# A scan-and-mixer kernel: the sums of WQ's columns in two rounded products, ten preparatory products, the order made anew

## The chip, the cores and the metric

The kernel runs on one core of a Trainium2 chip. The core has five queues that matter here: TensorE (PE in the profile, with its weight loads as PEld), VectorE (DVE), ScalarE (ACT), GpSimd (POOL, which also issues the accumulating transfers) and SyncE (SP, which issues the other transfers). The metric is the device time of one execution in microseconds. Before the change it is 519.17 us, the median of 3 runs from 518.96 to 519.18.

## The reference

```python
x  = A_x                                # 1 x 2048 x 512, float32
xn = layernorm(x)                       # eps 1e-5
# A: linear attention, 32 heads of 16
q, k, v = heads(xn @ wqkv)
phi = lambda t: where(t > 0, t + 1, exp(t)) + 1e-6
pq, pk = phi(q), phi(k)
kv  = einsum("bhsd,bhse->bhde", pk, v);  z = einsum("bhsd->bhd", pk)
s   = (einsum(pq, kv) / (einsum(pq, z)[..., None] + 1e-6)) @ wo
# B: spatial-shift mixer, then an MLP 512 -> 1376 -> 512
h   = gelu(layernorm(xn) @ w1)
x1  = xn + shifted(h) @ w2              # four channel groups, shifted by +1, -1, +2, -2
m   = x1 + gelu(layernorm(x1) @ w3) @ w4
return x + s * silu(m)
```

All inputs and the output are float32. The products have to be more exact than one product of rounded operands gives.

## The kernel before, in words

Rows are tiled by 128, so there are 16 row tiles; four of them make a block, and there are four blocks. Columns and inner dimensions are cut into chunks of 128 (four for 512).

TensorE has two kinds of product. A native float32 product (`slow=True` in `mm`, line 141) runs in two passes. A rounded product takes operands of type float32r. To keep the precision, an operand is split into a rounded part `hi` and a rest `lo`: `rounded` (line 478) is one ACT copy into `hi` and one VectorE subtraction into `lo`. A product of two split operands is then three rounded products, hi with hi, hi with lo and lo with hi (`products`, line 470).

The layer norm ahead of wqkv isn't applied to the rows before the product. The raw rows, transposed on the host, are multiplied, and the mean is corrected afterwards: `sums` (line 680) adds the four chunks of a weight matrix with three VectorE additions into one tile t, multiplies a matrix of ones by t, which leaves the sums of all columns in every row of a PSUM bank, and an ACT copy negates them into `wneg` (for the keys) or `qneg` (for the queries). The first step after each product of rows and weights is then `t = wneg * mean + product` (`feature_k`, line 739, and `query`, line 765) on VectorE, and ACT scales by the inverse deviation. W1's columns are centered in a like way by `center` (line 561), whose sum is already taken in two rounded products.

The work runs in this order. Preparatory products (`warm`, line 1168) use TensorE until the first weights land. Then come the keys of block 0 (the first two tiles with a native product of the unrounded first chunk), the sums of WK's columns, the load and split of WQ, the sums of WQ's columns, and from there queries, keys, and `gram` (line 776), which accumulates the keys' features against the normalized rows in four PSUM banks. The halves of a key's features and of its normalized rows are k0h, k0l, x0h, x0l and so on. For the mixer, `mix1` multiplies shifted blocks by w1, `mix2` multiplies by w2 in the form of `seven` (line 783), which gets a 2x2 block product from seven products instead of eight, with VectorE additions between them. Behind row tile 15 the attention matrices are closed, and then the MLP runs block by block: `up_pair` in sevens, `down` into four accumulator banks (`acc`), the attention's products in sevens (`attend_pair`), and `gate` at the block's end. The rows of y, which feed `up_pair`, go through DRAM to be turned: `Turned.put` stores them, `Turned.take` fetches them in four transfers per half block (line 715).

None of this order is the order of execution. Each operation is entered in a plan with an estimated duration, and `emit` (line 267) writes out all five queues by simulating them: it takes the next operation by its due time (`deadlines`, `backward`), gives tiles their buffers, and assumes transfer times. What it writes is static; on the chip each queue runs in the order written and waits where an operand isn't there. The numbers that steer it are these: the allowance for a transfer in the due time (6.0 us plus 4 us per MB, line 265), `SAFE` (line 230), the margin that a reader gets behind the assumed landing of its transfer, `lead` and `reserve` (in the call of line 1409), how early a tile of a class may be taken and how many free ones lengthen that, and `SOONER` (line 1401), a table of pairs: operation number, and by how many quarters of a microsecond its due time is brought forward. Operation numbers count the operations in the order entered, so an operation that is added moves the numbers behind it.

There are four PSUM banks for products (`mm`) and four for accumulators (`acc`), and 90 buffers of class "p" in SBUF for most of the tiles.

Of the kernel before, what the change touches and what calls it, by code (L numbers as in the profile page):

```python
# [85 lines left out]
class Plan:  # L86
# [140 lines left out]
    GAP = .06  # L227
    PATIENCE = 2.5
    COLD, COLD_TILL = 1.84, 5.8
    SAFE = 2.0  # L230
    early = 0.0
    patience = 18.0

# [27 lines left out]
    def backward(self):  # L261
        for op in reversed(self.ops):
            if op.eng != "PE":
                for o in op.post:
                    op.due = min(op.due, o.due - self.GAP - (6.0 + op.mb * 4 if op.mb else op.lat))

    def emit(self, first, lead, reserve, window, ahead, table=()):
        self.deadlines(first)
# [19 lines left out]
        while left:  # L288
# [86 lines left out]
            for o in op.post:  # L375
# [7 lines left out]
                if op.mb:  # L383
                    r = max(r, min(r + self.SAFE, o.due + slip - o.lat - self.SAFE))
                o.ready = max(o.ready, r)
# [8 lines left out]
def linear_attn_gated_by_mixer(  # L394
# [24 lines left out]
    W = 4  # L419
    SHIFT = (-1, 1, -2, 2)  # L420
    ORDER = (0, 2, 1, 3)
    WARM = 8
    PIECE = BT + W
    EARLY = (), ()
    AHEAD = 30.0, 20.0, 10.0, 0.0, 0.0
# [12 lines left out]
    pl = Plan(nc, pools, counts, ("acc", "mm"))  # L438

    def piece(name, dt=F32):  # L440
        return pl.new("p", name, dt, PIECE)[:, :512]

    def rounds(name):

        return piece(name + "h", F32R), piece(name + "l", F32R)
# [4 lines left out]
    def bank(name):  # L450
        return pl.new("mm", name, F32, 512)[:, :]

    def fixed(name, n, dt=F32):

        t = pl.new("const", name, dt, n)
        t.ap = const.tile([P, n], dt, name=name)
        return t
# [9 lines left out]
    def split(out, full, hi):  # L467
        pl.tt(out, full, hi.f32, ALU.subtract)
# [9 lines left out]
    def rounded(hi, lo, full, src=None):  # L478

        pl.act(hi, src or full, AF.Copy)  # L480
        split(lo, full, hi)
# [9 lines left out]
    ident, ones, nhalf, zacc = fixed("ident", P), fixed("ones", P), fixed("nhalf", QT), fixed("zacc", 512)  # L491
    identr = fixed("identr", P, F32R)
    onesr, bmask, tiny, zmore = fixed("onesr", P, F32R), fixed("bmask", P), fixed("tiny", 1), fixed("zmore", 1)
# [186 lines left out]
    def sums(w, ps, out):  # L680

        t, r = piece(f"{w.name}t"), w.raw
        pl.tt(t, r[0], r[1], ALU.add)
        pl.tt(t, t, r[2], ALU.add)
        pl.tt(t, t, r[3], ALU.add)
        pl.mm(ps, ones.all, t, True, True, slow=True)
        pl.act(out, ps, AF.Copy, scale=-1.0)


# [478 lines left out]
    warm = bank("warm")  # L1168
    for n in range(WARM):
        pl.mm(warm.cols(n % NC * P, (n % NC + 1) * P), ones.all, ones.all, True, True, slow=True)  # L1170
# [18 lines left out]
    WK = Weights("wk", wqkv[1])  # L1189
# [17 lines left out]
    for i in range(2):  # L1207
        project(ks[i], i, WK, [3])
    sums(WK, ksum, wneg)
    for i in range(2):  # L1210
        feature_k(i, ks[i])
# [3 lines left out]
    WQ = Weights("wq", wqkv[0])  # L1215
    WQ.split()
    sums(WQ, bank("qsum"), qneg)
    query(0)
    gram(0)
# [77 lines left out]
    for base, s in ((0, 1), (DH - 1, -1)):  # L1297
        v = bmask.all.via(lambda ap: ap.rearrange("p (h d) -> p h d", d=DH))
# [16 lines left out]
    for gg in range(NC):  # L1315
        cs = gg * P, (gg + 1) * P
        ps = bank(f"kv{gg}").cols(0, P)
# [4 lines left out]
    for gg in range(NC):  # L1322
        ps = bank(f"m{gg}")
# [10 lines left out]
    for b in range(NQ):  # L1334
# [46 lines left out]
        else:  # L1381
# [3 lines left out]
            t = piece(f"xi{i}", F32R)  # L1385
# [13 lines left out]
                gate(b * QT + QT - 1, a, o, D // 2, late=True, by_dma=False, whole=o > 0)  # L1399

    SOONER = (
# [6 lines left out]
    )  # L1408
    pl.emit(first=6.0, lead={"p": 14.0, "w": 14.0, "ab": 10.0}, reserve={"p": 20, "w": 1, "ab": 0}, window=12.0,
            ahead=6.0, table=SOONER)  # L1410


# [35 lines left out]
```

## Time and profile before

| what | value |
|---|---|
| median of 3 runs | 519.17 us (518.96 to 519.18) |
| profiled execution | 519.35 us, of it 517.6 us span |
| mean granted TensorE clock | 0.998 |
| busy: TensorE / weight loads | 511.2 / 445.0 us |
| busy: VectorE / ACT / POOL | 394.0 / 324.8 / 102.8 us |
| DMA | 100.12 MB, mean 193 GB/s |

The span runs from the first to the last instruction; the rest of the profiled execution's time lies around it. A product on TensorE is shown with its whole passage through the array, so that successive products overlap in the profile: a busy TensorE doesn't tell that it runs at its peak, and a short gap doesn't show in the busy time. The distance from one start to the next does. The two passes of a native product are two instructions. In the rows of the timeline and of the chain the first number is the start in us, the second the duration; an arrow reads "out from in"; a bracket tells how long the engine was idle before and who ended that.

### The profile page before, as it was taken

How to read it: one execution, taken by the hardware profiler on the slowest of the kernel's cores; microseconds unless marked ns; L12 is line 12 of the kernel's file. 1: busy time of each engine (PE TensorE's matmuls, PEld its weight loads, DVE VectorE, ACT ScalarE, POOL GpSimd, SP SyncE). 2: the span in 40 equal slices, each digit the busy share in tenths (PEclk: the TensorE clock that was granted, in tenths of full speed). 3: DMA queues.
4: the chain of work that ended last, by engine and by line, in shares of the span. 5: the costliest groups of instructions: out<-in, count | busy, mean ns of one | idle time of the engine just before them, and what ended most of it. 6: DMA issues, size and time to landing. Idle time of an engine off the chain costs nothing.

```text
span 517.6 us, 8927 instructions
## 1 busy us (share of the span) xinstructions
PE 511.2 (99%) x3005; PEld 445.0 (86%) x3005; DVE 394.0 (76%) x788; ACT 324.8 (63%) x664; POOL 102.8 (20%) x195
## 2 busy tenths in 40 slices
PE   8999999999999999999999999999999999999996
PEld 6777888988888888898889989899898898999985
DVE  5884987569567838999999999655886657895635
ACT  5899784579558657787866755345453545535621
POOL 1378643431363022211100001000020000200000
PEclk9999999999999999999999999999999999999999
DMA  8759994375976389989767759648488376687604
GB/s 277 255 101 248 225 205 97 74 172 182 220 169 162 68 185 249 259 261 262 287 200 225 237 175 249 212 152 208 133 214 276 122 201 157 179 248 225 243 1 122
DMA packets 73281, 100.12 MB, mean 193 GB/s; under 512 B 7844, under 2 KB 30900, under 8 KB 73236
## 3 DMA queue, kind: packets, MB, share of 16 engines
q1 hardware_dynamic: 63876, 82.52, 50.6%
q0 software_dynamic: 9360, 17.04, 19.9%
q8 instruction: 23, 0.38, 0.3%
q14 instruction: 22, 0.18, 0.1%
HBM read 60.33 MB, written 30.81 MB: 176 GB/s over the span
## 4 chain that ended last, share of the span: by engine, by line
PE 91%; ACT 5%; DVE 2%; DMA 1%; issue 1%; SPq 0%; DVEq 0%
PE acc L146 22%; PE pb L146 10%; PE k L146 8%; PE h L146 8%; PE q L146 7%; PE g L146 7%; PE pe L146 5%; PE pbs L146 5%; PE pbm L146 4%; PE pa L146 3%; PE pes L146 2%; PE a L146 2%; PE pem L146 2%; PE pas L146 1%; ACT y L167 1%; PE pam L146 1%
## 5 line engine op out<-in xcount | busy, mean ns | idle before, releaser
L223 POOL DMA_DIRECT2D th<-in_x x14 | 12.2, 919 | 247.3 <-PE a L146 126.2
L167 ACT ACTIVATE p<-pb 128x256 f32<-128x256 f32 x20 | 7.7, 385 | 25.8 <-PE pb L146 25.4
L223 POOL DMA_DIRECT2D o<-x x16 | 15.0, 935 | 40.4 <-DVE o L189 19.7
L223 POOL DMA_DIRECT2D zacc<-kr x16 | 14.6, 910 | 41.8 <-DVE kr L199 33.6
L167 ACT ACTIVATE th<-xo 128x512 f32<-128x512 f32 (+1 forms) x16 | 9.7, 619 | 19.3 <-DVE xo L189 16.2
L167 ACT ACTIVATE gf<-gf 128x512 f32<-128x512 f32 (+1 forms) x40 | 20.9, 523 | 0.8
L223 POOL DMA_DIRECT2D pqd<-qe x16 | 14.7, 921 | 28.9 <-ACT p5m L167 10.0
L167 ACT ACTIVATE p<-pe 128x256 f32<-128x256 f32 x20 | 7.7, 386 | 18.9 <-PE pe L146 18.9
L189 DVE TENSOR_TENSOR xo<-acc,xo 128x512 f32<-128x512 f32 (+1 forms) x16 | 10.3, 670 | 11.4 <-PE acc L146 11.4
L199 DVE SCALAR_TENSOR_TENSOR kt<-wneg,mv,k 128x512 f32<-128x512 f32 x16 | 11.9, 742 | 9.4 <-PE k L146 8.5
L199 DVE SCALAR_TENSOR_TENSOR kr<-kt,kr 128x512 f32<-128x512 f32 x16 | 11.0, 690 | 10.4 <-ACT kt L167 10.4
L199 DVE SCALAR_TENSOR_TENSOR qt<-qneg,mv,q 128x512 f32<-128x512 f32 x16 | 11.9, 742 | 7.2 <-PE q L146 7.1
L167 ACT ACTIVATE ht<-ht 128x512 f32<-128x512 f32 x16 | 10.0, 630 | 11.5 <-DVE ht L189 11.4
L189 DVE TENSOR_TENSOR gf<-u,pe 128x256 f32<-128x256 f32 x20 | 8.3, 416 | 11.2 <-PE pe L146 11.2
L189 DVE TENSOR_TENSOR gf<-pa,p 128x256 f32<-128x256 f32 x20 | 8.4, 418 | 10.5 <-PE pa L146 10.4
L189 DVE TENSOR_TENSOR ht<-h,abc 128x512 f32<-128x512 f32 x16 | 10.8, 686 | 6.5 <-PE h L146 6.5
L167 ACT ACTIVATE x<-x,nm,rs 128x512 f32<-128x512 f32 x16 | 12.5, 802 | 2.9 <-POOL nm L189 2.9
L167 ACT ACTIVATE qr<-qt,rs 128x512 f32<-128x512 f32 x16 | 11.4, 715 | 4.1 <-DVE qt L199 4.1
L590 DVE BATCH_NORM_STATS2 st<-o 128x6 f32<-128x512 f32 x16 | 10.9, 683 | 1.8 <-DMA o<-x 1.8
L167 ACT ACTIVATE kr<-kt,rs 128x512 f32<-128x512 f32 x16 | 11.4, 715 | 1.2 <-DVE kt L199 1.1
L167 ACT ACTIVATE y<-o,nm,rs 128x512 f32<-128x512 f32 x16 | 12.0, 805 | 0.1
L167 ACT ACTIVATE kt<-kt,rs 128x512 f32<-128x512 f32 x16 | 11.4, 715 | 0.1
(1559 smaller groups left out, 2195.9 us busy)
## 6 DMA issues: line engine op xcount, KB each, us to landing
w_s<-in_w SPq DMA_DIRECT2D x28, 256.0 KB, 5.5
x<-in_x SPq DMA_DIRECT2D x16, 256.0 KB, 5.2
zacc<-kr POOLq DMA_DIRECT2D x16, 256.0 KB, 3.9
pqd<-qr SPq DMA_DIRECT2D x16, 256.0 KB, 3.3
pqd<-qe POOLq DMA_DIRECT2D x16, 256.0 KB, 5.4
o<-x POOLq DMA_DIRECT2D x16, 256.0 KB, 4.6
x1d<-o SPq DMA_DIRECT2D x16, 256.0 KB, 4.9
pq<-pqd SPq DMA_DIRECT2D x16, 256.0 KB, 6.0
```

The source lines that it names most:

```text
L146: lambda: nc.tensor.matmul(out.get(), lhs.get(), rhs.get(), start=start, stop=stop, skip_group_check=more))
L167: nc.scalar.activation(out.get(), src.get(), func, scale=get(scale), **kw)
L189: self.vec(eng, out, [a, b], lambda: self.e(eng).tensor_tensor(out.get(), a.get(), b.get(), op=op), True)
L199: lambda: self.nc.vector.scalar_tensor_tensor(out.get(), a.get(), get(s), b.get(), op0=op0, op1=op1),
L223: lambda: self.nc.gpsimd.dma_start(out.get(), get(src), accum_op=ALU.add), mb=mb)
L590: pl.add("DVE", .62, .69, [xv], [st], lambda: nc.vector.bn_stats(st.get(), xv.get()))
```

## The change

In `sums`, the tile t of WQ is split into its rounded part and its rest, and the matrix of ones (rounded, `onesr`) is multiplied by each of the two into the same bank. That is one ACT copy, one VectorE subtraction and two rounded products in place of one native product. WK's sums stay native. The preparatory products are ten instead of eight. `SAFE` is 1.0 instead of 2.0, the allowance for a transfer 5.0 us instead of 6.0 (plus 4 us per MB), the lead of class "p" 12 us instead of 14, its reserve 26 instead of 20, and the table `SOONER` is another one, with numbers that fit the added operations. With that, all queues are written in a new order.

```diff
-    SAFE = 2.0
+    SAFE = 1.0
...
-                    op.due = min(op.due, o.due - self.GAP - (6.0 + op.mb * 4 if op.mb else op.lat))
+                    op.due = min(op.due, o.due - self.GAP - (5.0 + op.mb * 4 if op.mb else op.lat))
...
-    WARM = 8
+    WARM = 10
...
         pl.tt(t, t, r[3], ALU.add)
-        pl.mm(ps, ones.all, t, True, True, slow=True)
+        if w is WK:
+            pl.mm(ps, ones.all, t, True, True, slow=True)
+        else:
+            ts = rounds(f"{w.name}m")
+            rounded(*ts, t)
+            for n, v in enumerate(ts):
+                pl.mm(ps, onesr.all, v, n == 0, n == 1)
         pl.act(out, ps, AF.Copy, scale=-1.0)
...
     SOONER = (
-        19, 20867, 20, 10505, 21, 8920, 22, 8153, 23, 20874, 26, 12597, 28, 17, 29, 8881, 34, 1005, 35, 11144,
...
+        21, 21508, 22, 10669, 23, 8995, 24, 8189, 25, 21479, 28, 12818, 31, 8848, 36, 1056, 37, 11477, 63, 30,
+        79, 21, 139, 1082, 141, 182, 146, 57, 158, 34, 179, 149, 181, 160, 183, 192, 185, 191, 189, 170, 253, 2,
...
-    pl.emit(first=6.0, lead={"p": 14.0, "w": 14.0, "ab": 10.0}, reserve={"p": 20, "w": 1, "ab": 0}, window=12.0,
+    pl.emit(first=6.0, lead={"p": 12.0, "w": 14.0, "ab": 10.0}, reserve={"p": 26, "w": 1, "ab": 0}, window=12.0,
             ahead=6.0, table=SOONER)
```

9 rows, old and new, of the table SOONER are left out of this document.

## The prediction

> **What bounds the kernel now.** I read the page first: busy shares, the slices, the chain that ended last.
>
> ```profile
> span 517.6 us, 8927 instructions
> PE 511.2 (99%) x3005; PEld 445.0 (86%) x3005; DVE 394.0 (76%) x788; ACT 324.8 (63%) x664; POOL 102.8 (20%) x195
> ...
> PE   8999999999999999999999999999999999999996
> ...
> PE 91%; ACT 5%; DVE 2%; DMA 1%; issue 1%; SPq 0%; DVEq 0%
> ```
>
> TensorE is the bound: 511.2 of 517.6 us, nine tenths or more in every slice but the first and the last, and 91% of the chain. A change can gain by less work on TensorE or by shorter gaps there, and lose by new gaps; what another engine does counts only where TensorE waits for it. The profiled execution took 519.35 us, 1.75 us beyond its span; the median of the runs is 519.17, 0.18 lower. I add all terms to the profiled execution and give the result against the median, that is 0.18 lower.
>
> The 5% of ACT in the chain is one stretch, which the chain in order of time shows; the busy time by stretches stands below it.
>
> ```profile
> 15.73 0.60 ACT wneg L167
> ...
> 22.94 0.52 ACT u_2h L167
> 23.46 0.52 ACT u_1h L167
> 23.98 0.52 ACT u_0h L167
> ...
> 28.46 0.53 ACT x1h L167
> 28.98 0.04 issue
> 29.03 3.05 PE g L146 x12
> 32.08 1.84 PE q L146 x8
> ```
>
> ```profile
> 16.00:28.00 12.00, 12.00 (x50) 9.00 (x49) 10.89 (x26) 12.00 (x27) 3.19 (x7) 1.00 0.54 172
> 48.00:64.00 16.00, 16.00 (x72) 12.92 (x70) 14.13 (x23) 12.83 (x24) 10.73 (x25) 1.00 0.97 236
> ```
>
> The columns are stretch, length, and busy time of PE, PEld, DVE, ACT and POOL. From 16 to 28 us ACT is busy in all 12.00 us and VectorE in 10.89; from 48 on ACT has 3 us in 16 free. The product for the sums of WQ's columns lies inside the full stretch.
>
> Last, the gaps of TensorE itself. Products are pipelined, so a gap is not read from the busy time but from the distance of two starts: 0.23 us for a rounded 512-column product, 0.12 for 256 columns. Beyond that, there are five waits of some size:
>
> ```profile
> 28.54 0.40 PE L146 MATMUL q<-wq_1h,u_1h 128*128 128x512 f32 x1
> 29.03 0.97 PE L146 MATMUL g<-k1h,x1h 128*128 128x512 f32 x3
> ...
> 33.53 0.39 PE L146 MATMUL q<-wq_3h,u_3l 128*128 128x512 f32 x1
> 33.94 1.20 PE L146 MATMUL g<-k2h,x2h 128*128 128x512 f32 x4
> ...
> 221.59 0.28 PE L146 MATMUL pbm<-w_t2h,hs23l 128*128 128x256 f32 x1
> 222.15 0.38 PE L146 MATMUL pem<-w_b22h,hs43h 128*128 128x256 f32 x1 [0.28 <-ACT p5m L167]
> 222.37 0.28 PE L146 MATMUL pem<-w_b22l,hs43h 128*128 128x256 f32 x1
> ...
> 262.83 0.40 PE L146 MATMUL acc<-w_1l,f_1h 128*128 128x512 f32 x1
> 263.30 0.39 PE L146 MATMUL pb<-yt40h,w_b 128*128 128x256 f32 x1
> ...
> 483.20 0.28 PE L146 MATMUL pbs<-m_t2h,q12s0l 128*128 128x256 f32 x1
> 483.48 0.39 PE L146 MATMUL pes<-m_b22h,q12s1h 128*128 128x256 f32 x1
> ```
>
> Start to start less the usual distance: 0.49 - 0.23 = 0.26, 0.41 - 0.23 = 0.18, 0.56 - 0.12 = 0.44, 0.47 - 0.23 = 0.24 and 0.28 - 0.12 = 0.16, together 1.28 us. The product behind a wait comes late too: 222.37 - 222.15 is 0.22, not 0.12. At 0.1 for each wait that is 0.5 more, so 1.8 us is what another order can take out here. It is also the measure of what a new order can put in.
>
> **The change, part by part.**
>
> *The native product for the sums of WQ's columns.*
>
> ```profile
> 20.39 0.40 PE L146 MATMUL q<-wq_3h,u_3h 128*128 128x512 f32 x1
> 20.68 1.13 PE L146 MATMUL qsum<-wqt,ones 128*128 128x512 f32 x2
> 21.24 0.80 PE L146 MATMUL q<-wq_3l,u_3h 128*128 128x512 f32 x1
> 21.88 0.40 PE L146 MATMUL q<-wq_3h,u_3l 128*128 128x512 f32 x1
> 22.11 0.40 PE L146 MATMUL g<-k0h,x0h 128*128 128x512 f32 x1
> ```
>
> From 20.39 to 22.11 TensorE takes 1.72 us for three rounded products, which would need 3 x 0.23 = 0.69, and the native one: 1.03 us for that one, with its two passes, a wait of 0.06 before it and a slow return to rounded products behind it (21.24 to 21.88 is 0.64 where 0.23 is usual). Two rounded products take 2 x 0.23 = 0.46. Gain: 1.03 - 0.46 = 0.57 us of TensorE. [...]
>
> *The rounding that feeds them.* It adds one ACT copy and one VectorE subtraction of 128x512. The same operations on WQ's chunks, and the reader of the sums:
>
> ```profile
> 13.02 0.62 ACT L167 ACTIVATE wq_1h<-wq_s 128x512 fp32r<-128x512 f32 x1
> 14.36 0.68 DVE L189 TENSOR_TENSOR wq_1l<-wq_s,wq_1h 128x512 fp32r<-128x512 f32 x1
> 23.85 0.74 DVE L199 SCALAR_TENSOR_TENSOR qt<-qneg,mv,q 128x512 f32<-128x512 f32 x1
> ```
>
> One after another they put the sums' product 0.62 + 0.68 = 1.3 us later than the sum's readiness, so the sums stand at about 22 us and not 20.7. On full ACT a copy takes 0.52 us of the queue (23.46 to 23.98). Behind it in ACT's queue stand x0h, k0h and later x1h, for which TensorE waits at 29.03; behind the subtraction stand the lows k0l and x0l. The sums' negation and then qt at 23.85 come later by up to 1.3 us, and with qt one PSUM bank of four. I cost all of this at nothing, for two covers. The three copies u_2h, u_1h, u_0h (1.56 us) are ahead of x1h in ACT's queue, and u's second block is first multiplied by key(4), behind g's and q's products. And TensorE has eight products of q (1.84 us at 32.08) that stand behind g's and could go before them. Without these covers, the copy's 0.52 us lands on x1h, and TensorE reaches its wait 0.57 us sooner for nothing.
>
> *Ten preparatory products.*
>
> ```profile
> 1.12 3.78 PE L146 MATMUL warm<-ones 128*128 128x128 f32 x16 [1.12 <-POOL ones L503]
> 5.27 2.60 PE L146 MATMUL k<-wk_s,xt 128*128 128x512 f32 x4 [0.37 <-DMA wk_s<-in_wqkv]
> ...
> 7.94 0.40 PE L146 MATMUL k<-wk_0l,u_0h 128*128 128x512 f32 x1
> ```
>
> Sixteen passes (eight products) end at 4.90, the last taking 0.42, so they start (3.78 - 0.42)/15 = 0.22 us apart. Four more end TensorE's part at about 4.48 + 5 x 0.22 = 5.6, past the 5.27 at which wk's first chunk lets it go: +0.33 us if nothing else changes. But from 5.27 to 7.94 TensorE takes 2.67 us for two native products and a rounded one, which at 0.97 (the 1.03 above without its wait) and 0.23 would take 2 x 0.97 + 0.23 = 2.17: 0.50 us is lost to a slow array. With the gap filled the array may be fast by 5.6, which gives 5.6 + 2.17 = 7.77: -0.17. Between the ends -0.17 and +0.33 I take +0.1, about the middle, since products that start later have less of the slow stretch in front of them.
>
> [...]
>
> *The planner's numbers and the table.* With the allowance for a transfer cut from 6.0 to 5.0 us plus 4 us per MB, the margin behind a landing from 2.0 to 1.0, the lead of "p" tiles from 14 to 12, its reserve from 20 to 26, and a new table, every queue is made anew: TensorE's, ACT's, VectorE's, POOL's with its accumulating transfers, SP's with all loads and stores. No operation is added by that; which step is moved past which isn't to be read from the trace of before. I bound it by the gaps: -1.8 us if all five waits and their late restarts go, and as upper end the rival on transfers below, +3.0. I take half of the removable: -0.9. The two waits of the stretch from 28 to 34 us have the covers named; the other three are single operands that arrive 0.16 to 0.44 late, and rows next to them (acc products) are there to fill.
>
> Sum: -0.57 + 0 + 0.1 - 0.9 = -1.4 us; 519.35 - 1.4 = 517.95 for a profiled execution, 517.8 against the median.
>
> **The rivals.**
>
> *The gain is given back at the next wait (within 0.2%).* TensorE comes to x1h 0.57 us sooner, ACT brings it 0.52 later, and the other waits return elsewhere in the same number. For it: the chain runs through ACT without a break from 15.73 to 28.98. Against it: the two covers. Time: between -0.57 + 0.33 = -0.24 and +0.52, that is 518.9 to 519.7.
>
> *Transfers land behind their readers (slower).* The place is the fetch of the turned rows y.
>
> ```profile
> y_1t<-y_1d SPq DMA_DIRECT2D x16, 128.0 KB, 5.9
> ```
>
> ```profile
> DMA to landing us min/median/max: 3.8/5.9/6.9
> ```
>
> ```profile
> ACT yb122h L167 <- DMA y_1t<-y_1d: 0.7, 1, 0.7
> ACT yb121h L167 <- DMA y_1t<-y_1d: 0.5, 1, 0.5
> ```
>
> These 0.13 MB fetches were allowed 6.0 + 0.5 = 6.5 us and now 5.5, while the median landing takes 5.9 and the slowest 6.9; ACT already waits for them twice. A fetch issued 1.0 us later with its reader placed 1.0 sooner blocks ACT's queue at each of the three later blocks, behind it the roundings and GELUs of the running block, and TensorE once its few acc products are gone. At 1.0 us for each block: +3.0 - 0.47 = +2.5, 521.7. It decides from 1.5 us of TensorE standing in all, which eats the 0.47 and passes 0.2%. Against it: a due time only ranks a fetch, which goes when its tile and queue are free, and TensorE doesn't wait for any fetched tile now. [...]
>
> *The order as a whole is worse placed (slower).* The seven-product blocks each wait for VectorE ahead of their last product; ten more waits of the size of 262.83's, 0.24 + 0.1, are +3.4 - 0.47: 522.1.
>
> **How the numbers follow.** Some 0.2% (1.04 us) is about what a measurement of this kernel tells from no change. The forecast (faster, 516.6 to 518.1) has 0.45; the gain given back 0.29; late transfers 0.16; the worse order 0.10. So 0.45, 0.29 and 0.26. The lower end is all that can be gained, -0.57 - 0.17 - 1.8 = -2.5: 516.6. The upper end lets in most of the transfers' rival and not its full price: 521.0. The forecast's own range is 516.6 to 518.1, the number 517.8.
>
> **What would show it.** The changed profile should have two products for the sums 0.23 us apart with no slow one behind them; one copy and one subtraction for them, finished between 20 and 23 us; twenty passes at the start and the first key product at 5.5 to 5.6, the second rounded one at 7.8 to 8.3; the waits of gram at 29 and 34 us below 0.2. It is wrong if TensorE waits for x1h or x2h by 0.5 us or more, if waits for y's roundings or for products of fetched tiles appear behind 290 us, or if the gaps behind 200 us sum to more than the 0.84 now seen in three.

## The result, and the profile after

The changed kernel takes 520.17 us in the median (519.32 to 521.31, 20 runs), the kernel before, beside it, 519.28 us (518.76 to 521.34, 20 runs). The ratio is 1.0018 with a 95% interval of 1.0011 to 1.0025: slower by 0.9 us. That is inside the 0.2% that I called no change, but surely not the gain of 1.4 us that I forecast. The executions spread by some 2 us, so times are compared below by medians of many runs. A timeline or a list of waits is always that of one execution.

The page of the changed kernel: the span, the busy time, the chain that ended last.

```profile
span 517.5 us, 8903 instructions
PE 511.2 (99%) x3009; PEld 445.7 (86%) x3009; DVE 394.0 (76%) x789; ACT 325.9 (63%) x667; POOL 104.4 (20%) x195
...
PE 88%; ACT 5%; DMA 4%; DVE 2%; issue 0%; SPq 0%
```

TensorE is the bound as before. The span is as long as before (517.6) and so doesn't show the loss, for two reasons. First, this profiled execution took 519.92 us, so 2.4 us lie around its span, where the kernel before had 1.75; in the median it is 2.39 (20 runs) against 1.72 (29 runs of the kernel before in the first set of experiments). So 0.67 us of the 0.9 lie outside the span, in a place that my sum held fixed. Second, the profiled span is shorter than the usual one: the median span of the changed kernel is 517.8 us (516.9 to 518.9), that of the kernel before in those 29 runs 517.5. And the chain now has 4% of DMA, where it had 1%. What that costs isn't told by the share: the run a_q14 below has 6% in its profile and is shorter.

Two answers of the timeline of TensorE, the start of the kernel and the place of the exchange (start, duration, operation, and in brackets the wait before):

```profile
1.58 4.64 PE L146 MATMUL warm<-ones 128*128 128x128 f32 x20 [1.58 <-POOL ones L503]
6.01 2.06 PE L146 MATMUL k<-wk_s,xt 128*128 128x512 f32 x4
...
8.13 0.40 PE L146 MATMUL k<-wk_0l,u_0h 128*128 128x512 f32 x1
...
19.33 0.39 PE L146 MATMUL q<-wq_0h,u_0l 128*128 128x512 f32 x1
...
21.19 0.40 PE L146 MATMUL q<-wq_3l,u_3h 128*128 128x512 f32 x1
21.64 0.50 PE L146 MATMUL qsum<-wqmh,onesr 128*128 128x512 f32 x1
21.98 0.39 PE L146 MATMUL q<-wq_3h,u_3l 128*128 128x512 f32 x1
22.25 0.96 PE L146 MATMUL g<-k0h,x0h 128*128 128x512 f32 x3
23.05 0.39 PE L146 MATMUL qsum<-wqml,onesr 128*128 128x512 f32 x1
23.28 0.40 PE L146 MATMUL g<-k0l,x0h 128*128 128x512 f32 x1
...
33.80 0.40 PE L146 MATMUL q<-wq_3h,u_3l 128*128 128x512 f32 x1
```

The slow return behind the native product, 0.64 us from start to start before, is gone: behind the two sums products the next ones start 0.34 and 0.23 us later. But seven products from 21.19 to 23.28 take 2.09 us, where 7 x 0.23 would be 1.61: 0.48 us went into late operands. The list of waits of the weight loads between 19 and 38 us (in total, times, longest):

```profile
PEld qsum L146 <- ACT wqmh L167: 0.5, 1, 0.5
PEld g L146 <- ACT x1h L167: 0.4, 1, 0.4
PEld g L146 <- ACT k0h L167: 0.3, 1, 0.3
PEld g L146 <- DVE x1l L189: 0.3, 1, 0.3
```

The first sums product waits for ACT's copy `wqmh`, and gram behind it for k0h; these two lie in the stretch. The other two waits, for x1h and x1l, come at 28 and 29 us. All come from the two queues that the copy and the subtraction lengthened. The weights of a product are loaded here while the one before it still runs (those of q's, from 21.74 us for 0.19, under the first sums product, from 21.64 for 0.50), so a part of these waits is covered: 0.5 and 0.3 us in the list, 0.48 us lost.

### The profile page after: what moved, and what is told of

Same layout as the page of the kernel before. It is cut to its first block, busy times and chain, and to the rows that moved or that the text cites. A ratio compares the mean times of both kernels' runs of the same rounds, so it can differ in the third digit from the quotient of the medians.

```text
span 517.5 us, 8903 instructions
## 1 busy us (share of the span) xinstructions
PE 511.2 (99%) x3009; PEld 445.7 (86%) x3009; DVE 394.0 (76%) x789; ACT 325.9 (63%) x667; POOL 104.4 (20%) x195
## 4 chain that ended last, share of the span: by engine, by line
PE 88%; ACT 5%; DMA 4%; DVE 2%; issue 0%; SPq 0%
PE acc L146 23%; PE pb L146 11%; PE g L146 8%; PE q L146 7%; PE k L146 6%; PE pe L146 6%; PE h L146 5%; PE pbs L146 4%; PE pbm L146 4%; PE pa L146 3%; PE pes L146 2%; PE a L146 2%; PE pem L146 2%; DMA x<-in_x 1%; PE pas L146 1%; DMA zacc<-kr 1%
```

## The experiments

In these kernels all queues are written in a recorded order, so that the planner moves nothing else: that of the changed kernel where the name begins with a, that of the kernel before where it begins with b. (a_pad_dve and a_pad_act are planned as the changed kernel is; what they add lies outside the plan.) The runs were made in three sets, each with its own runs of the kernel before (median spans 517.5, 517.9 and 517.7 us). The spans in this table are medians, less the median of the kernel before in the same set; for the change, less the 517.5 us of the first set. Around the span, the kernel before has 1.72 to 1.73 us in every set. Of the ratios, which compare times, those of the change and b_qsum lie clear of 1 as slower, those of a_nat_all, a_all and, barely, a_nocopy as faster; the intervals of the others cover or touch 1.

| run | edit | time, us | ratio to before (95%) | span | around the span |
|---|---|---|---|---|---|
| the change | | 520.17 | 1.0018 (1.0011 to 1.0025) | +0.3 | 2.39 |
| a_native | native product back | 518.91 | 0.9992 (0.9977 to 1.0006) | -0.75 | 2.16 |
| b_qsum | order before, exchange alone | 521.23 | 1.0027 (1.0016 to 1.0039) | +1.6 | 1.69 |
| a_nocopy | sums products without copy and subtraction | 518.89 | 0.9989 (0.9979 to 0.9999) | -0.7 | 1.89 |
| b_warm10 | order before, ten preparatory products alone | 519.10 | 0.9995 (0.9984 to 1.0006) | -0.5 | 1.71 |
| a_ones | `ones` cleared first | 520.23 | 1.0012 (1.0000 to 1.0024) | +0.3 | 2.41 |
| a_pad_dve | 12 instructions more on VectorE | 519.68 | 1.0008 (0.9997 to 1.0018) | +0.1 | 2.06 |
| a_pad_act | 12 instructions more on ACT | 519.33 (one run) | not told by one run | | 2.03 |
| a_nat_pads | native product, both additions | 519.13 | 0.9990 (0.9976 to 1.0004) | -0.45 | 1.71 |
| a_q14 | q14t fetched earlier | 519.32 | 0.9991 (0.9980 to 1.0001) | -0.8 | 2.17 |
| a_nat_all | native, q14t, `ones`, both additions | 518.66 | 0.9987 (0.9978 to 0.9996) | -0.8 | 1.71 |
| a_all | exchange kept, the rest as a_nat_all | 518.71 | 0.9983 (0.9969 to 0.9997) | -0.7 | 1.71 |

My theory was that the exchange saves 0.57 us because its copy and subtraction are hidden. The rival was the first one of the prediction: ACT's copy lands on TensorE.

### The exchange undone in the changed order

```diff
-        if w is WK:
-            pl.mm(ps, ones.all, t, True, True, slow=True)
-        else:
-            ts = rounds(f"{w.name}m")
-            rounded(*ts, t)
-            for n, v in enumerate(ts):
-                pl.mm(ps, onesr.all, v, n == 0, n == 1)
+        pl.mm(ps, ones.all, t, True, True, slow=True)
```

> The changed kernel in its own recorded order with the native product back in the place of the first rounded one, and without the copy, the subtraction and the second product; all else is that of the changed kernel. Theory (the exchange gains 0.57 on TensorE, of which the wait for the rounded part and a late neighbour take 0.33 in the changed kernel): slower by 0.2 to 0.3 us in the span. Rival 1 (all of 0.57 reaches the end): slower by 0.5 to 0.6. Rival 2 (ACT's extra copy costs what TensorE gains): the same or faster by up to 0.3.

The median is 518.91 us (518.16 to 520.77), 1.26 us less than the change: 1.05 in the span, more than any of the three expectations had, and 0.23 around it. Of the weight loads' waits from 19 to 38 us one is left that has a releaser, and none for ACT:

```profile
PEld g L146 <- DVE x1l L189: 0.2, 1, 0.2
```

The cost is read best as the time between two products that both kernels have, the last of wq_0 in one pass over q and the last of wq_3 two passes later. In the changed kernel it is 33.80 - 19.33 = 14.47 us. With the native product:

```profile
19.28 0.39 PE L146 MATMUL q<-wq_0h,u_0l 128*128 128x512 f32 x1
...
21.13 0.39 PE L146 MATMUL q<-wq_3l,u_3h 128*128 128x512 f32 x1
21.37 1.02 PE L146 MATMUL qsum<-wqt,ones 128*128 128x512 f32 x2
21.82 0.79 PE L146 MATMUL q<-wq_3h,u_3l 128*128 128x512 f32 x1
22.45 0.85 PE L146 MATMUL g<-k0h,x0h 128*128 128x512 f32 x3
...
33.36 0.39 PE L146 MATMUL q<-wq_3h,u_3l 128*128 128x512 f32 x1
```

That is 14.08 us, so the exchange costs 0.39 on the spot in place of saving 0.57. The native product itself costs less than I took: from 21.13 to 22.45 stand two rounded products and it, 1.32 - 0.46 = 0.86 us, not 1.03. And 2 x 0.23 for its successors leaves 0.40 to gain at best.

In these two executions the loss reaches the end. At 29 us the changed kernel is 0.45 us behind (29.41 against 28.96, a product of k1l and x1h), 0.05 of it from ahead of the exchange, and at TensorE's last product 0.63 us. The changed kernel, and with the native product:

```profile
512.71 0.28 PE L146 MATMUL accx<-w_9h,f_9l 128*128 128x256 f32 x1
```

```profile
512.08 0.28 PE L146 MATMUL accx<-w_9h,f_9l 128*128 128x256 f32 x1
```

That x1h comes late is not for want of free time on ACT. ACT's row in the changed kernel, and with the native product:

```profile
23.14 0.72 ACT L167 ACTIVATE sq<-x,sx 128x512 f32<-128x512 f32 x1 [0.94 <-DVE sx L194]
```

```profile
22.69 0.73 ACT L167 ACTIVATE sq<-x,sx 128x512 f32<-128x512 f32 x1 [0.82 <-DVE sx L194]
```

In both kernels ACT stands idle here for VectorE's sx. With the exchange ACT's copy brings k0h 0.33 us later (21.48 against 21.15 us). In VectorE's queue the subtraction stands ahead of k0l, which needs k0h and starts 0.46 us later (22.36 against 21.90), and sx stands behind k0l. So ACT goes on 0.45 us later, and x1h starts at 27.59 us instead of 27.14. The delay passes through both queues.

### The exchange alone in the order before

The queues in words (in the kernel the order is a recorded table):

```diff
 ACT:     ... k0h, x0h
+ACT:     wqmh <- wqt
 ACT:     x1's squares
-ACT:     qneg <- qsum
 ACT:     u_2h, u_1h, u_0h, kr
+ACT:     qneg <- qsum
 VectorE: ... x0l
+VectorE: wqml <- wqt, wqmh
 VectorE: kt
-VectorE: qt <- qneg
 VectorE: sx, u_2l, u_0l
+VectorE: qt <- qneg
 TensorE: ... q <- wq_3h,u_3h
-TensorE: qsum <- wqt,ones (native)
 TensorE: q <- wq_3l,u_3h ... g <- k0h,x0l
+TensorE: qsum <- wqmh,onesr
 TensorE: g <- ... (the rest of block k0)
+TensorE: qsum <- wqml,onesr
```

> The exchange alone, in the order of the kernel before: ScalarE's copy behind x0h's, VectorE's subtraction behind x0l's, the two rounded products among the q products at the places that the native one and its neighbours had; everything else at its old place. My first account (the native product's 1.03 us is saved and the copy lies under others): span 516.9 us, time 518.7 us. The rival, read off the run of the changed kernel with the native product put back (the copy and the subtraction push the roundings behind them, and TensorE waits for x1h longer than it saves): span 518.0 to 518.5 us, time 519.8 to 520.3 us. If the cost is one of the changed order only, there is no difference beyond 0.3 us either way. About 1.72 us are to lie outside the span, as before, since ScalarE's and VectorE's lists keep their lengths within one or two instructions.

521.23 us (520.72 to 521.89), 1.6 us more span than before: 519.5 us, where my rival ended at 518.5. TensorE's own waits from 19 to 38 us, without those of its weight loads; the kernel before has none there in this list:

```profile
PE g L146 <- ACT x1h L167: 0.8, 1, 0.8
PE g L146 <- DVE x0l L189: 0.6, 1, 0.6
PE g L146 <- ACT x0h L167: 0.6, 1, 0.6
```

and ACT in the same kernel:

```profile
26.08 0.60 ACT L167 ACTIVATE qneg<-qsum 128x512 f32<-128x512 f32 x1 [0.65 <-PE qsum L146]
...
29.92 0.62 ACT L167 ACTIVATE x1h<-x 128x512 fp32r<-128x512 f32 x1
```

This shows two things that my sum left out. The native product was itself a cover: without it TensorE reaches gram 1 us sooner (at 21.11 us, where the kernel before starts it at 22.11) and stands there 0.56 us for x0h and 0.58 for x0l, which nothing makes earlier. And the sums now come late, ACT stands 0.65 us for them ahead of their negation, the copy has taken 0.52 more, and x1h starts at 29.92, not 28.36. I chose the places of the four new instructions here, and with them the sums' negation and the first qt were moved behind u's rounding. So 1.6 us is the price of these places, not the least price of the exchange.

### The two products without the copy and the subtraction

```diff
-            ts = rounds(f"{w.name}m")
-            rounded(*ts, t)
-            for n, v in enumerate(ts):
+            for n, v in enumerate(w.hl[3]):
                 pl.mm(ps, onesr.all, v, n == 0, n == 1)
```

> The changed kernel in its own recorded order, but the two rounded sums products take the two parts of WQ's fourth chunk, which are long there, in place of the rounded sum and its rest; ScalarE's copy and VectorE's subtraction are left out. So the column sums of Q are those of one chunk (left out of the computation: the sum over the four). If the copy on ScalarE is the whole cost of the exchange: no wait at the first sums product nor at x1h, TensorE done 0.3 to 0.6 us earlier than with the native product (span 516.2 to 516.5 us against 516.75, time 518.4 to 518.6 with 2.16 us outside the span). If the two products cost what they save whatever feeds them: span 516.75 us, time 518.9 us. If the copy had no part in it: span 517.8 us as in the changed kernel, time 520.2 us.

```profile
19.25 0.39 PE L146 MATMUL q<-wq_0h,u_0l 128*128 128x512 f32 x1
...
33.01 0.39 PE L146 MATMUL q<-wq_3h,u_3l 128*128 128x512 f32 x1
```

The stretch takes 13.76 us: 0.32 less than with the native product, 0.71 less than with the exchange. So the products do save, and ACT's copy with VectorE's subtraction, the wait for the copy included, costs twice what they save. In the profiled execution the lead over the native product is kept to TensorE's last product (0.37 us, 511.72 against 512.08). The medians don't show it: 518.89 us against 518.91, and a span of 517.0 us where I had expected 516.2 to 516.5. They come from two sets, and runs that spread by more than 1.5 us don't tell 0.3.

### The preparatory products alone

```diff
-    WARM = 8
+    WARM = 10
```

> Two more preparatory products alone, in the order of the kernel before. If they only lie in time in which the first key product waits for the chunks' sum: the same time, 519.25 us. If they hold the first key product back by what they last (2 x 0.23 us): 519.7 us. If the array is fast earlier for them, as the second rounded pass of the changed kernel suggests (2.06 us for four products against 2.60): 518.9 us.

```profile
1.11 4.64 PE L146 MATMUL warm<-ones 128*128 128x128 f32 x20 [1.11 <-POOL ones L516]
5.54 2.61 PE L146 MATMUL k<-wk_s,xt 128*128 128x512 f32 x4
...
8.23 0.39 PE L146 MATMUL k<-wk_0l,u_0h 128*128 128x512 f32 x1
```

The second rounded key product starts at 8.23, not 7.94: 0.29 us later, near my upper end of 0.33, and the array is no faster for the two products (the natives take 2.61 us, before 2.60). My reason for +0.1, that products which start later have less of the slow stretch in front of them, this trace doesn't show: the natives start 0.27 us later and last as long. At the end of the kernel nothing is left of the 0.29: the ratio's interval covers 1.

### What clears `ones` late

In the changed order GpSimd clears the accumulator's zero tile, 0.52 us, ahead of `ones`, and the preparatory products start at 1.58 instead of 1.12 us. Nothing in the steering numbers says so; it came with the new order. The queue in words:

```diff
 GpSimd:
-    zacc <- 0
     ones <- 1
+    zacc <- 0
```

> The changed kernel in its own recorded order, with one step moved: the memset of zacc behind those of ones and ident, as before the change. The first preparatory product then starts at 1.12 and not at 1.58 us. Theory (the late start is carried to the end, since TensorE is the bound): the span falls by 0.3 to 0.46. Rival (the first weights and the array's slow stretch set the start of the real products, not the preparatory ones): by less than 0.1.

```profile
1.11 3.92 PE L146 MATMUL warm<-ones 128*128 128x128 f32 x20 [1.11 <-POOL ones L516]
...
7.24 0.40 PE L146 MATMUL k<-wk_0l,u_0h 128*128 128x512 f32 x1
```

The second rounded product is 0.9 us sooner here (7.24 against 8.13), a part of it because the twenty passes took 3.92 us in this execution and 4.64 in the changed kernel's. At 482 us the lead is 0.34 us (482.55 against 482.89, the last product ahead of the wait below), and in the median nothing of it is left: 520.23 us. The profiled execution is the slowest of the twelve (521.19 us). In it the lead is lost, and 0.87 us more, at one place, the fetch of q14's turned rows. The answer on the tile q14t (us, times; then the time from issue to landing), the waits of TensorE from 478 to 493 us, and the tile's landing in the kernel before:

```profile
who waited for it (us, times):
  DVE q14f L189: 3.0, 1
  ACT q14h L167: 1.2, 1
...
DMA to landing us min/median/max: 5.8/5.8/5.8
```

```profile
PE pes L146 <- ACT p5s L167: 1.2, 1, 1.2
```

```profile
DMA to landing us min/median/max: 2.2/2.3/2.5
```

The chain is plain: q14t lands late, ACT stands at q14h, behind q14h in ACT's queue stands p5s of another product, and TensorE waits 1.2 us for p5s. A lead won earlier only brings TensorE sooner to this wait. The new order has stored q15 ahead of q14 and issues q14t behind 1.3 MB that nobody needs soon. SP in the changed kernel:

```profile
471.60 0.38 SPq L210 DMA_DIRECT2D q14d<-q14z  x1
472.07 0.38 SPq L217 DMA_DIRECT2D xo<-x1d  x1
...
474.01 0.42 SPq L217 DMA_DIRECT2D w_7l<-w4d  x1
474.53 1.79 SPq L217 DMA_DIRECT2D q14t<-q14d  x4
```

The landing takes 5.8 us here (5.3 in the changed kernel) against 2.3 before, where q14t was ahead of the same transfers.

### q14t ahead of the transfers that can wait

The queue in words:

```diff
 SyncE:
     q14d <- q14z
-    xo <- x1d; w_2h, w_2l, w_7h, w_7l <- w4d
     q14t <- q14d (four fetches)
+    xo <- x1d; w_2h, w_2l, w_7h, w_7l <- w4d
```

> The changed kernel in its own recorded order, but SP issues the four fetches of q14t directly behind q14d's store, ahead of one xo fetch and of w_2h, w_2l, w_7h and w_7l (1.3 MB), whose readers come 10 us later and more. If these transfers ahead of it in the queue are why q14t lands late and why the span of the changed order spreads from 516.9 to 518.9 us: q14t lands in under 3.5 us, the waits of q14f and q14h are gone, span 517.0 to 517.3 us in the middle, time 519.4 to 519.7 us. If the spread has another cause: 520.2 us with the same spread.

```profile
DMA to landing us min/median/max: 1.8/2.8/3.8
```

That is the landing of q14t in this kernel, and nobody waits for it any more. The median span is 517.1 us, 0.7 less than the change; against the kernel before it is 0.8 us shorter, where the change was 0.3 longer. So the late fetch costs the changed kernel 0.7 to 1.1 us in the median. The spans of the changed kernel reach from 516.9 to 518.9 us, these from 516.7 to 517.8: the long ones are gone, as far as eleven runs tell. It is what stands ahead in the queue that counts, and not the moment of issue: in a_all below, q14t is issued no sooner than in the changed kernel (from 474.6 us on, against 474.5) and lands in 1.9 to 3.3 us, against 5.3.

### What lies around the span

Two runs add instructions that compute nothing to the heads of two queues of the changed kernel.

```diff
+    for _ in range(12):
+        nc.vector.memset(mv2.ap[:, 0:1], 0.0)
     pl.emit(...)
```

> The changed kernel with twelve one-column memsets more at the head of VectorE's list, where VectorE waits for its first transfer anyway. The executions of the changed kernel take 2.4 us beyond their span, the one of before 1.75, and in the trace of before a piece of instructions (8192 bytes) is fetched at 513.9 us that the changed kernel doesn't fetch in its span. Theory (a list of instructions that ends just ahead of the place where its next piece is fetched leaves that fetch to the end of the execution): VectorE's list has 1085 profiled instructions against 1094, and the fetch at 513.9 came at its 1088th; with twelve more the fetch returns into the span and the part outside falls from 2.4 to about 1.75, the time by 0.65. Rival (the list is another engine's, ACT's above all, or the 0.65 has to do with the last transfers): the part outside stays at 2.4 and the time at that of the changed kernel.

```diff
     pl.act(onesr.all, ones.all, AF.Copy)          # shortened: written in emit, behind this copy
+    for _ in range(12):
+        nc.scalar.activation(onesr[:, :1], ones[:, :1], AF.Copy)
```

> The changed kernel with twelve one-column copies more in ACT's list, behind its first copy, ahead of the first landed weights. If ACT's list is the one that ends short of its next piece (826 profiled instructions at 513.9 us before, 823 in all after), the part outside the span falls from 2.4 to about 1.75 us here and not with VectorE's memsets. If it is VectorE's list or the transfers, it stays at 2.4.

2.39 us around the span become 2.06 with the one and 2.03 with the other: 0.33 and 0.36 less, half of the 0.65 that I expected from one list alone. With both (a_nat_pads, a_all, a_nat_all) it is 1.71, the 1.72 of the kernel before. My idea was that the place counts where a piece of a list's code is fetched. The queue "instruction" (packets, MB, share) from 513.4 to 514.6 us, in the kernel before and with the additions on VectorE:

```profile
q14 instruction: 1, 0.01, 1.6%
```

```profile
q14 instruction: 1, 0.01, 2.1%
```

The changed kernel has no such packet there, so the additions on VectorE did bring a piece of 0.01 MB back to this place. But the time around the span doesn't follow the packets. With the additions on ACT there is none in this stretch either, and the time is 2.03 us; in a_all there is none, and it is 1.71. Behind the last instruction one is fetched in the kernel before (at 518.9 us) as in the changed one (at 519.1), and none with the additions on VectorE, which still have 2.06 us. So the two additions move the time around the span, and how they do it isn't shown.

More instructions aren't the rule either. Counted with those that the page leaves out, the profile has 1085 instructions on VectorE and 823 on ACT in the changed kernel, 1085 and 822 in a_native, 1084 and 822 in a_nocopy, 1087 and 823 in a_q14; these three have 2.16, 1.89 and 2.17 us. What is waited for behind the last instruction stays open.

> The changed kernel in its own recorded order with the native product put back (no copy, no subtraction), and twelve one-column instructions more at the head of VectorE's list and twelve in ScalarE's, whose results nobody reads. If 0.33 us outside the span belong to each of the two lists (the last piece of each list's code is fetched behind the end): about 1.7 us outside the span, the span as with the native product alone (516.75 us), time 518.4 to 518.6 us, faster than both kernels. If the outside time belongs to something else: 518.9 us, as without them, or more by what the added instructions cost.

Its 1.71 us are as expected. Its span isn't: the median is 0.45 us below that of the kernel before, not 0.75, and the time 519.13 us where 518.4 to 518.6 were expected; one run has a span of 519.6 us. In that execution VectorE waits 1.5 us for q14t and 2.2 us for another late fetch:

```profile
DVE qz L199 <- DMA pq<-pqd: 2.2, 1, 2.2
...
PE pb L146 <- DVE gf L189: 1.1, 1, 1.1
```

### All repairs, with and without the exchange

> The changed kernel's order with the native product put back, q14t's fetches ahead of the xo and w transfers, zacc's clearing behind ones, and the twelve one-column instructions more on VectorE and on ScalarE. If the causes found so far add up (native product -1.05 us of span, q14t -0.6 us and the long runs gone, outside the span 1.71 us): span 515.9 to 516.4 us, time 517.6 to 518.1 us, faster than both kernels by 0.2% and more. If they overlap (the late wait swallows what is gained ahead of it): span 516.7 us, time 518.4 us.

> The same with the exchange kept as in the changed kernel: q14t's fetches ahead, zacc's clearing behind ones, the instructions added on VectorE and ScalarE. Against the run with the native product it shows what the exchange costs once nothing else differs: 0.5 to 1.05 us of span more by the account of ScalarE's copy (span 516.7 to 517.1 us, time 518.4 to 518.8 us); 0.57 us less by my first account (span 515.5 us, time 517.2 us).

518.66 us (518.17 to 519.58) and 518.71 us (518.35 to 519.58): with both, the order, mended in four places, is faster than the kernel before by 0.13% and 0.17%, and 1.5 us faster than the change as it was made (across two sets of runs). At the end the exchange makes no difference that these runs can tell (median spans 516.9 and 517.0 us), neither the 0.5 to 1.05 of my expectation nor a gain of 0.57. On the spot it still costs:

```profile
18.87 0.39 PE L146 MATMUL q<-wq_0h,u_0l 128*128 128x512 f32 x1
...
32.91 0.39 PE L146 MATMUL q<-wq_3h,u_3l 128*128 128x512 f32 x1
```

```profile
18.90 0.39 PE L146 MATMUL q<-wq_0h,u_0l 128*128 128x512 f32 x1
...
33.18 0.40 PE L146 MATMUL q<-wq_3h,u_3l 128*128 128x512 f32 x1
```

14.04 us with the native product and 14.28 with the exchange: +0.24. The gains don't add up as I had written in the expectation (515.9 to 516.4 us of span): repairing q14t and putting the native product back take out the same loss in the medians, and only once.

## Why the prediction was wrong

I forecast -1.4 us and got +0.9. By its steps:

- *The exchange, -0.57.* Wrong in sign. On the spot it costs 0.39 us in the changed order. Two parts of the step failed. The native product was sized at 1.03 us, at a place where its own operand wqt comes late: it starts 0.06 us late there and lasts 0.56 to the next start (20.68 to 21.24), in the changed order 0.45 (21.37 to 21.82). There it costs 0.86, so 0.40 was to be had at most, and 0.32 was had. And the copy and subtraction, costed at nothing, cost 0.71 us: without them the stretch is 13.76 us, with them 14.47.
- *The covers.* I named two. u's copies no longer stand between x0h and x1h in ACT's queue, as I had hoped, but the first sums product waits for the copy itself (0.5), which no cover ahead of x1h can help. The q products do stand ahead of gram, and x1h still is late (0.4). I had the right rival for this ("the gain is given back at the next wait"), with 0.29: its place is right, and x1h starts 0.45 us later where it had 0.52. Its mechanism is right only in part, since the delay passes through VectorE's queue too and ACT stands idle meanwhile. Its range, 518.9 to 519.7, is missed for what lies around the span.
- *The reading of the chain.* I took the 5% of ACT in the chain before for one stretch. From 15.73 to 28.98 us it is 13.0 us; 14.1 us more lie between 200 and 300 us, where I had looked at single gaps only.
- *Ten preparatory products, +0.1.* Between -0.17 and +0.33 the trace of b_warm10 says +0.29 at 8 us, and its runs say nothing that can be told from zero at the end. The row that my lower end reckoned with, the second rounded product at 7.77 us on an array that is fast by 5.6, isn't there. That later products have less of the slow stretch in front of them was my estimate, and the runs show no such order: the first four native passes took 1.96 us from 5.21 on (a_ones), 2.42 (a_all) and 2.61 (b_warm10) from 5.54, 2.06 from 6.01 (the changed kernel). The first key product is at 5.54 us in b_warm10, where I had 5.5 to 5.6. In the changed kernel it is at 6.01, because `ones` is cleared 0.46 us later, a move in GpSimd's queue that I didn't look for.
- *The order, -0.9.* About right in sum, as far as it can be told: with the native product back the span is 0.75 us below that of the kernel before, by twelve spans that reach from 516.0 to 518.6 us. The native kernel in this order also has the two preparatory products in it. Of the waits that I listed, in the changed kernel k2h's and pb's are gone, x1h's is down to 0.13 (27.91 to 28.27), pem's to 0.24, and pes's stayed. But the same order brought the late q14t, which with the exchange takes the gain away again.
- *Transfers that land behind their readers.* The rival's mechanism is real: a fetch that lands late, its reader blocking ACT's queue, and behind it something that TensorE needs. I put it at y's fetches; it is at q14t, once and not three times, and costs 0.7 to 1.1 us, not 3. And I argued from the allowance alone; what makes q14t late is what stands ahead of it in SP's queue.
- *The time around the span, held at 1.75.* It grew by 0.67 us, most of the 0.9, and I held it fixed without a reason. Twelve more instructions on each of two engines bring it back; by what way stays open.

In sum: exchange with q14t late +1.05 (517.8 - 516.75, across two sets of runs), order and preparatory products -0.75, around the span +0.67, that is +0.97, against +0.9 measured. The three add up by the way they were taken, so the sum proves nothing. How much of the +1.05 is the exchange and how much q14t can't be split in the medians, since either repair alone takes out most of it; in the two profiled executions the exchange accounts for 0.4 of 0.63. Why q14t's wait bites less in the kernel with the native product (its landing was 4.3 us in the one profile, 5.3 in the changed kernel's) isn't settled.

## What to carry to other kernels

A product on the bound engine that is replaced by a cheaper one with more preparation isn't cheaper where the preparation stands in the queues that bring the next operands, even if an engine there has idle time (here 0.32 us saved and 0.71 spent, with ACT idle for 0.94 us): follow the next operand back through all queues that it passes. The replaced product may also have been the cover of a late one (b_qsum: 0.56 and 0.58 us of new waits). In a new order look first at what stands ahead of each fetch in its queue and at whose queue its reader blocks, because one such fetch can swallow every gain made earlier (a_ones: a lead of 0.34 us, and 0.87 more). And keep the time around the span as a term of its own when differences of 0.1% are at stake.

## What the runs showed of the hardware that I had not expected

Twelve instructions that compute nothing, added to VectorE's list, made the execution 0.33 us shorter outside the span, and twelve on ACT 0.36 us; why isn't shown. The same four fetches of 64 KB landed in 4.3 (a_native) to 5.8 us (a_ones) with 1.3 MB of other transfers ahead of them in the queue, and in 1.8 to 3.8 us ahead of those (a_q14). And the same twenty preparatory passes took 3.92 us in one profiled execution (a_ones) and 4.63 to 4.64 in three others (the changed kernel, a_all, b_warm10), with the first native products 1.96 to 2.61 us long: how fast the array runs at the start differs by execution; why isn't shown.
